# Chunked attention and a top-2 expert layer: two heads in one 128-row product, values loaded a batch ahead, routing work moved on VectorE

## The chip, the cores and the metric

One core of a Trainium2 chip runs the whole program. The metric is device time in microseconds (us) of one launch, from the program's start to its end; the median of several launches is given. A core has five engines that run side by side, each through its own stream of instructions in order: TensorE (PE in the profile; its weight loads are PEld), VectorE (DVE), ScalarE (ACT), GpSimd (POOL) and SyncE (SP). SP, ACT and POOL also issue DMA transfers. Waits between engines and transfers go through semaphores.

## What is computed

Attention in chunks (batch 4, 8 heads, 768 tokens, head width 64): each chunk of 32 queries sees 8 memory keys, 16 tokens to the left, its own 32 and 8 to the right, 64 keys in all. The result, seen as 3,072 rows of 512, goes through a layer of 8 experts of which each row takes the two best by noisy logits.

```python
for c in range(nc):                       # 24 chunks of 32
    k_full = np.concatenate([mem_k, k[:, :, l_start:r_end]], axis=2)
    v_full = np.concatenate([mem_v, v[:, :, l_start:r_end]], axis=2)
    scores = scale * np.matmul(q_c, k_full.transpose(0, 1, 3, 2))
    a = np.exp(scores - np.max(scores, axis=-1, keepdims=True))
    a = a / (np.sum(a, axis=-1, keepdims=True) + 1e-09)
    out[:, :, c_start:c_end] = np.matmul(a, v_full)
...
noisy_logits = x @ w_gate + np.log1p(np.exp(x @ w_noise)) * noise
top2 = np.argpartition(-noisy_logits, 2, axis=1)[:, :2]
...                                       # weights w of the two: softmax over them
    h = np.maximum(x[mask] @ w1[e], 0.0)
    out[mask] += top2_w[mask, k, None] * (h @ w2[e])
```

## The kernel before

**Two halves.** The attention half runs in 12 slots (`i` = 0 to 11): batch `b = i // 3`, and in it `tp = i % 3`, two tiles of 128 tokens. The expert half walks 20 visits of an expert to blocks of 128-row slots, with `mm1` (L637) and `mm2` (L652).

**One slot.** PE first makes the scores of the *next* slot (`scores`, L380): for each tile and each pair of heads a product against the memory keys and four against the windows, and all of these once for each head of the pair (`par`), with 64 rows of contraction. DVE takes the maximum and subtracts it (L406, L408), ACT takes the exponential (L413). Then PE turns this slot's probabilities (`turn_p`, L420), ACT copies them out (L423); PE turns the previous slot's rows (`turn_x`, L457); `values` (L426) makes the sums (L431) and the product with the values (L439), once for each head again; DVE takes the reciprocal (L444) and scales into `xrow` (L447). `gate` (L462) makes logits of the previous slot. `ps_s` and `ps_o` have one buffer each; the PSUM pool `psT`, for everything that is turned, has three.

**Keys, queries, values of the next batch.** In the slot with `tp == 1` PE turns the next batch's keys (four pairs, `turn`, L374, copies L546), in the one with `tp == 2` its queries (copies L528). Values take a longer way: they land in `vn`, POOL reorders them into `vp` (`spread_v`, L349), SP writes `vp` to DRAM (`vd`, L355), and POOL issues the loads of the windows back into `vb` (`window_v`: L359 for the memory values, L364 for the windows).

**POOL's queue.** All loads of v, k, q, windows and expert weights are issued by POOL, in the order of the program, on one DMA queue; a wait of one holds up those behind it. At `tp == 0` the order is `window_v(b+1)`, `load_batch(b+2)` (v, k, q), `spread_v(b+2)`. In the slots 6, 7 and 8 `load_expert(0)`, `(1)`, `(2)` follow, each two transfers (L74 for w1, L75 for w2).

**Memory.** The attention half borrows from `w_all`, which later holds the eight experts' weights, 8,192 elements of a partition each. `scratch` hands out pieces from the top down: `xrow`, `vb`, `vp`, `vn`, then `nat`, the raw k and q, [batch parity][k or q], of which `nat[1][1]` (q of batches 1 and 3) comes last and lowest. That is 36,864 of 65,536 elements, so the lowest piece starts at 28,672, in expert 3 (24,576 to 32,767).

**Order.** PE, ACT, DVE and SP follow the order of the program text as it is written in the main loop; POOL's are pinned. A read of `w_all` waits for the last write in program order that overlaps it.

**Routing.** `route(b)` (L326) is a generator of five steps: `choose` (18 small DVE operations, L224 to L258), `ranks` (PE) and `weights` (seven small DVE operations), `place` and `total`, `values` and `slots` (L311, L306), `lists`. The main loop takes a step at a time between the other stages. After slot 11 the last batch's routing follows in two parts, then rows are gathered by expert pair (L607) and the expert half starts.

Of the kernel before, what the change touches and what calls it, by code (L numbers as in the profile page):

```python
# [22 lines left out]
def kernel(  # L23
# [76 lines left out]
    vb = [scratch(NCH * HP * D).rearrange("p (c w) -> p c w", c=NCH) for _ in range(2)][::-1]  # L100
    vp = scratch(H * SO * D)
    vn = scratch(H * SO * D).rearrange("p (h c) -> p h c", h=H)
    nat = [[scratch(H * SO * D).rearrange("p (h c) -> p h c", h=H) for _ in range(2)] for _ in range(2)]
    first_late = scol[0] // WE

# [5 lines left out]
    def load_batch(b):  # L111
        load_nat(vn, v, b)
        load_nat(nat[b % 2][0], k, b)
        load_nat(nat[b % 2][1], q, b)

    load_batch(0)
# [13 lines left out]
    zeros = keep.tile([LC, Dm], BF16, name="zeros")  # L130
# [10 lines left out]
    mvs = keep.tile([B * NM, H, D], F32, name="mvs")  # L141
# [53 lines left out]
    kT = [keep.tile([128, HP, SP], BF16, name=f"kT{i}") for i in range(2)]  # L195
    qT = [keep.tile([128, HP, S], BF16, name=f"qT{i}") for i in range(2)]
    for i in range(2):
        nc.vector.memset(kT[i][:, :, 0:LC], 0.0)
        nc.vector.memset(kT[i][:, :, LC + S:SP], 0.0)

    mkT = keep.tile([128, HP, B * NM], BF16, name="mkT")
# [6 lines left out]
    nc.vector.tensor_copy(mkT, p_mk.rearrange("p c x b m -> p c (x b m)"))  # L208
# [117 lines left out]
    def route(b):  # L326
        r = Route(b * SO, SO, lgs[b])
        r.noise()
        yield
        advance(r.choose())  # L330
        yield
        r.ranks()
        r.weights(nc.vector)
        yield
        advance(r.place())
        advance(r.total())
        yield
        eng = nc.vector if b < B - 2 else nc.gpsimd
        r.values(eng, 0, NV)
        r.slots(nc.vector)  # L340
        yield
        r.lists(0, NV)
        yield


# [7 lines left out]
    def window_v(b):  # L353
        t, o = vb[b % 2], vd[b % 2]
        nc.sync.dma_start(out=o[LC:LC + S, :].rearrange("(p s) c -> p (s c)", s=SO), in_=vp)  # L355
        for par in range(2):
            p0 = par * 64
            cols = slice(par * 256, (par + 1) * 256)
            pin(nc.gpsimd.dma_start(out=t[p0:p0 + NM], in_=mvn[b * NM:(b + 1) * NM, cols].unsqueeze(1).to_broadcast([NM, NCH, 256])))  # L359
        for par in range(2):  # L360
            p0 = par * 64
            cols = slice(par * 256, (par + 1) * 256)
            for r0, n in ((0, CH), (CH, WIN - CH)):
                pin(nc.gpsimd.dma_start(out=t[p0 + NM + r0:p0 + NM + r0 + n],  # L364
                                        in_=o[r0:r0 + S, cols].rearrange("(c k) w -> k c w", k=CH)[0:n]))


    def turn(b, unit):
# [3 lines left out]
        for s in range(SO):  # L372
            for par in range(2):
                nc.tensor.transpose(out=p_t[par * 64:par * 64 + 64, s, :],  # L374
                                    in_=src[:, 2 * pair + par, s * D:(s + 1) * D],
                                    identity=identb, tile_position=(0, par * 64))
        dst = qT[b % 2][:, pair, :] if x else kT[b % 2][:, pair, LC:LC + S]
        return dst.rearrange("c (p s) -> c p s", s=SO), p_t.rearrange("c s p -> c p s")

    def scores(t):  # L380
        b, tp = divmod(t, TP)
        q_, k_ = qT[b % 2], kT[b % 2]
        ps_s = psS.tile([128, 2, 2, HP, KW], F32, name="ps_s")
        for j in range(2):
            for pair in range(HP):
                tk = (2 * tp + j) * 128
                for par in range(2):
                    rows = slice(par * 64, par * 64 + 64)
                    nc.tensor.matmul(out=ps_s[:, par, j, pair, 0:NM], lhsT=q_[rows, pair, tk:tk + 128],  # L389
                                     rhs=mkT[rows, pair, b * NM:(b + 1) * NM], start=True, stop=True,  # L390
                                     tile_position=(par * 64, 0))
                for r in range(4):
                    for par in range(2):
                        rows = slice(par * 64, par * 64 + 64)
                        tr = tk + r * CH
                        nc.tensor.matmul(out=ps_s[r * CH:(r + 1) * CH, par, j, pair, NM:KW],  # L396
                                         lhsT=q_[rows, pair, tr:tr + CH],
                                         rhs=k_[rows, pair, tr:tr + WIN], start=True, stop=True,
                                         tile_position=(par * 64, r * CH))
        if tp == 0:  # L400
            nc.vector.memset(ps_s[0:CH, :, 0, :, NM:NM + LC], NEG)
        if tp == TP - 1:
            nc.vector.memset(ps_s[128 - CH:128, :, 1, :, KW - RC:KW], NEG)
        s3 = ps_s.rearrange("p a j c w -> p (a j c) w")
# [6 lines left out]
    def exps(sc):  # L411
        pb = work.tile([128, 2 * HP, 2, KW], BF16, name="pb")
        nc.scalar.activation(out=pb.rearrange("p x a w -> p a x w"), in_=sc.rearrange("p (a x) w -> p a x w", a=2),  # L413
                             func=Act.Exp, scale=scale)
# [11 lines left out]
    def values(t, pT, between=None):  # L426
# [6 lines left out]
        ps_o = psO.tile([128, 2, 2, HP, D], F32, name="ps_o")  # L433
        for j in range(2):
            for pair in range(HP):
                for r in range(4):
                    for par in range(2):
                        rows = slice(par * 64, par * 64 + 64)
                        nc.tensor.matmul(out=ps_o[r * CH:(r + 1) * CH, par, j, pair, :],  # L439
                                         lhsT=pT[rows, j * HP + pair, r * CH:(r + 1) * CH],  # L440
# [457 lines left out]
```

## Time and profile before

| | |
|---|---|
| median of 3 runs | 391.89 us (388.24 to 396.87) |
| the profiled execution | 393.52 us, of which the profile's span is 391.8 us |
| busy in the span | PE 307.5, PEld 199.1, DVE 169.3, ACT 120.2, POOL 129.5 us |
| last rows of the attention half scaled (L447 of slot 11) | 151.9 us after the span's start |
| first gather of rows for the experts (L607) | 164.2 us |
| granted TensorE clock, mean | 0.85 |

Rows of the profile name line, engine, operation and "out<-in"; then how many, busy time and mean duration in ns, then the idle time before them and what ended it. In the timeline a row starts with its start and its duration in us, and [4.44 <-issue] means 4.44 us of idle time that ended with nothing that the profile shows. The slices cut the span into 40 parts of 9.8 us; a digit is a busy share in tenths. A row of the table of stretches gives each engine's busy time in that stretch, the clock, the DMA share and the GB/s moved. The trace also lists each DMA packet with queue, size, start and duration; v, k and q travel in packets of 768 bytes, windows in 4,096, w1 in 2,048 and w2 in 1,024, so each transfer can be followed by size.

### The profile page before, as it was taken

How to read it: one execution, taken by the hardware profiler on the slowest of the kernel's cores; microseconds unless marked ns; L12 is line 12 of the kernel's file. 1: busy time of each engine (PE TensorE's matmuls, PEld its weight loads, DVE VectorE, ACT ScalarE, POOL GpSimd, SP SyncE). 2: the span in 40 equal slices, each digit the busy share in tenths (PEclk: the TensorE clock that was granted, in tenths of full speed). 3: DMA queues.
4: the chain of work that ended last, by engine and by line, in shares of the span. 5: the costliest groups of instructions: out<-in, count | busy, mean ns of one | idle time of the engine just before them, and what ended most of it. 6: DMA issues, size and time to landing. Idle time of an engine off the chain costs nothing.

```text
span 391.8 us, 8846 instructions
## 1 busy us (share of the span) xinstructions
PE 307.5 (78%) x3868; PEld 199.1 (51%) x3868; DVE 169.3 (43%) x393; ACT 120.2 (31%) x182; POOL 129.5 (33%) x168
## 2 busy tenths in 40 slices
PE   0267765866758455379999999999988999999991
PEld 0256654755646343246555446666445666555540
DVE  2345444867657369734123411595321134313230
ACT  1122633540452323013432143312224411244310
POOL 6353234325520003476236522063272023201122
PEclk9999965565585555559999999999999999999997
DMA  9999999999999992039999970712039941100012
GB/s 125 238 141 189 213 157 222 219 150 217 204 182 218 217 205 66 12 98 190 240 209 247 228 153 14 122 44 95 24 114 173 210 97 73 68 5 2 21 43 74
DMA packets 42957, 54.07 MB, mean 138 GB/s; under 512 B 7607, under 2 KB 33271, under 8 KB 42912
## 3 DMA queue, kind: packets, MB, share of 16 engines
q0 software_dynamic: 34240, 46.82, 66.1%
q10 hardware_dynamic: 7136, 3.02, 3.6%
q1 hardware_dynamic: 1536, 3.61, 2.5%
q8 instruction: 32, 0.52, 0.5%
q14 instruction: 13, 0.11, 0.1%
HBM read 70.39 MB, written 13.96 MB: 215 GB/s over the span
## 4 chain that ended last, share of the span: by engine, by line
PE 30%; issue 17%; DMA 5%; POOL 4%; DVE 3%; POOLq 1%
PE p_h L646 16%; PE p_y L655 12%; DMA out_dram<-y,main_dst 5%; POOL out_dram L613 2%; PE p_xt L627 1%; POOL xt L607 1%; DMA xt<-xd,main_src 1%; POOL w_all L771 0%; POOL w_all L770 0%; DVE w_all L447 0%; POOLq L893 0%; DVE oh_l L306 0%; DVE c L227 0%; DVE mm L224 0%; DVE c L229 0%
## 5 line engine op out<-in xcount | busy, mean ns | idle before, releaser
L655 PE MATMUL p_y<-w_all,h 128*128 128x512 bf16 x464 | 103.9, 379 | 2.4 <-ACT y L659 2.4
L646 PE MATMUL p_h<-xTt,w_all 128*128 128x384 bf16 (+2 forms) x640 | 102.3, 319 | 0.0
L646 PEld LDWEIGHTS <-w_all 128*128 128x128 bf16 x704 | 66.8, 99 | 38.0 <-issue 2.1
L634 ACT ACTIVATE h<-p_h 128x512 bf16<-128x512 f32 (+1 forms) x82 | 44.7, 545 | 102.9 <-PE p_h L646 90.7
L655 PEld LDWEIGHTS <-h 128*128 128x128 bf16 x464 | 44.9, 98 | 53.5 <-issue 2.7
L632 DVE TENSOR_SCALAR h<-p_h 128x512 bf16<-128x512 f32 (+1 forms) x50 | 31.3, 626 | 89.4 <-PE p_h L646 86.4
L613 POOL DMA_INDIRECT out_dram<-y,main_dst x28 | 31.1, 1110 | 104.1 <-DVE y L661 84.0
L661 DVE SCALAR_TENSOR_TENSOR y<-p_y,main_w,y 128x512 f32<-128x512 f32 x28 | 21.0, 750 | 37.4 <-PE p_y L655 32.3
L607 POOL DMA_INDIRECT xt<-xd,main_src x28 | 27.3, 975 | 25.4 <-PE p_xt L627 16.1
L396 PE MATMUL ps_s<-kT,qT 64*32 64x56 bf16 x768 | 24.3, 220 | 13.3 <-issue 13.3
L374 PE MATMUL p_t<-identb,w_all 128*64 128x128 bf16 x384 | 20.8, 295 | 15.4 <-DMA w_all<-in_k_dram 8.2
L659 ACT ACTIVATE y<-p_y,main_w 128x512 f32<-128x512 f32 x28 | 19.1, 687 | 41.0 <-PE p_y L655 35.1
L423 ACT COPY pT<-p_p 128x1024 bf16<-128x1024 bf16 x12 | 12.1, 1012 | 58.2 <-PE p_p L420 58.2
L374 PEld LDWEIGHTS <-w_all 128*64 128x64 bf16 x384 | 18.7, 160 | 16.5 <-DMA w_all<-in_k_dram 8.3
L349 POOL COPY w_all<-w_all 128x1536 bf16<-128x1536 bf16 x8 | 13.0, 1658 | 35.0 <-DMA w_all<-in_v_dram 35.0
L389 PE MATMUL ps_s<-mkT,qT 64*128 64x8 bf16 x192 | 17.9, 184 | 4.4 <-DVE sc L408 2.9
L364 POOL DMA_DIRECT2D w_all<-vd x16 | 11.9, 748 | 25.0 <-DMA vd<-w_all 25.0
L406 DVE TENSOR_REDUCE mx<-ps_s 128x16 f32<-128x1024 f32 x12 | 14.7, 1223 | 8.9 <-PE ps_s L396 8.6
L447 DVE TENSOR_TENSOR w_all<-ps_o,rs 128x512 bf16<-128x512 f32 x24 | 15.6, 686 | 6.6 <-PE ps_o L439 6.0
L439 PE MATMUL ps_o<-w_all,pT 64*32 64x64 bf16 x768 | 10.0, 233 | 9.8 <-issue 9.8
L396 PEld LDWEIGHTS <-qT 64*32 64x32 bf16 x768 | 11.8, 96 | 11.2 <-issue 9.6
L389 PEld LDWEIGHTS <-qT 64*128 64x128 bf16 x192 | 10.0, 100 | 14.2 <-issue 5.8
(163 smaller groups left out, 300.3 us busy)
## 6 DMA issues: line engine op xcount, KB each, us to landing
w_all<-in_moe_w_dram POOLq DMA_DIRECT2D x16, 1024.0 KB
w_all<-in_moe_w_dram POOLq DMA_DIRECT2D x8, 512.0 KB
w_all<-in_v_dram POOLq DMA_DIRECT2D x4, 768.0 KB
w_all<-in_k_dram POOLq DMA_DIRECT2D x4, 768.0 KB
w_all<-in_q_dram POOLq DMA_DIRECT2D x4, 768.0 KB
vd<-w_all SPq DMA_DIRECT2D x4, 768.0 KB, 7.4
w_all<-vd POOLq DMA_DIRECT2D x8, 384.0 KB
xd<-w_all ACTq DMA_DIRECT2D x11, 256.0 KB, 7.6
```

The costliest lines, as they stand in the source:

```text
L374: nc.tensor.transpose(out=p_t[par * 64:par * 64 + 64, s, :], in_=src[:, 2 * pair + par, s * D:(s + 1) * D], identity=identb, tile_position ...
L389: nc.tensor.matmul(out=ps_s[:, par, j, pair, 0:NM], lhsT=q_[rows, pair, tk:tk + 128], rhs=mkT[rows, pair, b * NM:(b + 1) * NM], start=True ...
L396: nc.tensor.matmul(out=ps_s[r * CH:(r + 1) * CH, par, j, pair, NM:KW], lhsT=q_[rows, pair, tr:tr + CH], rhs=k_[rows, pair, tr:tr + WIN], s ...
L447: nc.vector.tensor_tensor(out=xr[:, j, 0:Dm].rearrange("p (c a d) -> p a c d", c=HP, a=2), in0=ps_o[:, :, j], in1=bc(rs[:, j].rearrange("p ...
L607: i = nc.gpsimd.indirect_dma_start(out=xts[key].bitcast(I32), out_offset=None, in_=xd, in_offset=bass.IndirectOffsetOnAxis(ap=ix, axis=0))
L613: i = nc.gpsimd.indirect_dma_start(out=out, out_offset=bass.IndirectOffsetOnAxis(ap=ix, axis=0), in_=y, in_offset=None, bounds_check=N - 1 ...
L632: nc.vector.tensor_scalar(out=out_, in0=in_, scalar1=0.0, scalar2=None, op0=Alu.max)
L634: nc.scalar.activation(out=out_, in_=in_, func=Act.Relu)
L646: nc.tensor.matmul(out=o, lhsT=w(kp * F + f * 128, 128), rhs=x[:, kp], start=(kp == 0), stop=(kp == KP - 1))
L655: nc.tensor.matmul(out=p, lhsT=h[:, (f * n + j) * 128:(f * n + j + 1) * 128], rhs=w(KP * F + f * Dm, Dm), start=(f == 0), stop=(f == FB - 1))
L659: nc.scalar.activation(out=y, in_=p, func=Act.Copy, scale=weight)
L661: nc.vector.scalar_tensor_tensor(out=y, in0=p, scalar=weight, in1=y, op0=Alu.mult, op1=Alu.add)
```

## The change

**Products.** Keys are kept block-diagonal: `kT` gets a column block for each head of a pair, with zeros in the other head's 64 rows; so do `mkT` and `vb`, whose size doubles. One product with 128 rows of contraction then serves both heads: per slot 40 instead of 80 in `scores`, with 112 instead of 56 columns (16 instead of 8 for the memory keys), and 32 instead of 64 in `values`, with 128 instead of 64 columns. A turned key tile is copied in two halves of 64 partitions. `kT` and `qT` have one buffer each instead of two. The zeros are written once at the start by DVE and ACT.

**Loads.** `load_batch` is split. `load_v(2)` is issued after `spread_v(1)`, before the loop, and `load_v(b + 3)` at `tp == 0` behind `spread_v(b + 2)`. `vp` leaves `w_all` for a tile of its own, `mvs` moves into expert 0's place.

**Memory.** The borrowed pieces now take 46,080 elements, and the lowest, `nat[1][1]`, lies at 19,456 to 22,527: inside expert 2 (16,384 to 24,575), the first 1,024 elements in w1's part, the rest in w2's. The calls of `load_expert` stay as they were, `load_expert(2)` in slot 8 ahead of the turn of batch 3's queries in the same slot. So in program order that turn reads what `load_expert(2)` has written there instead of batch 3's queries, and as built its first group of transposes waits for w1 of expert 2 and the second for w2.

**Routing.** `route` goes; its steps stand in the loop behind each slot's scaled rows and logits. `choose` is cut in two (8 and 10 operations, slots `tp == 0` and `tp == 1`), `weights` and `values` come ahead of the scores of the slot `tp == 2`, `settle` behind its logits, `lists` one slot later. In slot 11 `weights` and `values` are POOL's.

```diff
-    vb = [scratch(NCH * HP * D).rearrange("p (c w) -> p c w", c=NCH) for _ in range(2)][::-1]
-    vp = scratch(H * SO * D)
     vn = scratch(H * SO * D).rearrange("p (h c) -> p h c", h=H)
+    vb = [scratch(2 * NCH * HP * D).rearrange("p (a c w) -> p a c w", a=2, c=NCH) for _ in range(2)][::-1]
     nat = [[scratch(H * SO * D).rearrange("p (h c) -> p h c", h=H) for _ in range(2)] for _ in range(2)]
     first_late = scol[0] // WE
+    mvs = w_all[0:B * NM, 0, 0:2 * H * D].bitcast(F32).rearrange("p (h d) -> p h d", h=H)
...
-    def load_batch(b):
+    def load_v(b):
         load_nat(vn, v, b)
+
+    def load_kq(b):
         load_nat(nat[b % 2][0], k, b)
         load_nat(nat[b % 2][1], q, b)
...
+    vp = keep.tile([128, H * SO * D], BF16, name="vp")
+    zeros = keep.tile([128, Dm], BF16, name="zeros")
...
+    kT = keep.tile([128, HP, 2, SP], BF16, name="kT")
+    qT = keep.tile([128, HP, S], BF16, name="qT")
+    for par in range(2):
+        nc.vector.memset(kT[own(par), :, 1 - par, :], 0.0)
+        nc.vector.memset(kT[own(par), :, par, 0:LC], 0.0)
+        nc.vector.memset(kT[own(par), :, par, LC + S:SP], 0.0)
+        nc.vector.memset(vb[0][own(par), 1 - par], 0.0)
+        nc.scalar.copy(vb[1][own(par), 1 - par].rearrange("p (x c) w -> p x (c w)", x=NCH // 2),
+                       zeros[own(par), :].unsqueeze(1).to_broadcast([64, NCH // 2, Dm]))
+    mkT = keep.tile([128, HP, 2, B * NM], BF16, name="mkT")
...
     def turn(b, unit):
...
+        i = p_t.rearrange("c s p -> c p s")
+        if x:
+            return [(qT[:, pair, :].rearrange("c (p s) -> c p s", s=SO), i)]
+        return [(kT[own(par), pair, par, LC:LC + S].rearrange("c (p s) -> c p s", s=SO), i[own(par)]) for par in range(2)]
...
     def scores(t):
...
-                for par in range(2):
-                    rows = slice(par * 64, par * 64 + 64)
-                    nc.tensor.matmul(out=ps_s[:, par, j, pair, 0:NM], lhsT=q_[rows, pair, tk:tk + 128],
-                                     rhs=mkT[rows, pair, b * NM:(b + 1) * NM], start=True, stop=True,
-                                     tile_position=(par * 64, 0))
+                nc.tensor.matmul(out=ps_s[:, j, pair, :, 0:NM], lhsT=qT[:, pair, tk:tk + 128],
+                                 rhs=mkT[:, pair, :, b * NM:(b + 1) * NM], start=True, stop=True)
                 for r in range(4):
...
+                    tr = tk + r * CH
+                    nc.tensor.matmul(out=ps_s[r * CH:(r + 1) * CH, j, pair, :, NM:KW], lhsT=qT[:, pair, tr:tr + CH],
+                                     rhs=kT[:, pair, :, tr:tr + WIN], start=True, stop=True, tile_position=(0, r * CH))
...
     def values(t, pT, between=None):
...
                 for r in range(4):
-                    for par in range(2):
-                        rows = slice(par * 64, par * 64 + 64)
...
+                    nc.tensor.matmul(out=ps_o[r * CH:(r + 1) * CH, j, pair], lhsT=pT[:, j * HP + pair, r * CH:(r + 1) * CH],
+                                     rhs=vb[b % 2][:, :, (tp * 2 + j) * 4 + r, pair * D:(pair + 1) * D],
+                                     start=True, stop=True, tile_position=(0, r * CH))
...
         for u in range(2 * HP):
-            o_, i_ = turn(0, u)
-            (nc.scalar.copy if u % 2 else nc.vector.tensor_copy)(o_, i_)
-        load_batch(1)
+            for n, (o_, i_) in enumerate(turn(0, u)):
+                (nc.scalar.copy if (u + n) % 2 else nc.vector.tensor_copy)(o_, i_)
+        load_v(1)
+        load_kq(1)
         spread_v(1)
+        load_v(2)
...
             if tp == 0 and b + 1 < B:
                 window_v(b + 1)
                 if b + 2 < B:
-                    load_batch(b + 2)
+                    load_kq(b + 2)
                     spread_v(b + 2)
+                if b + 3 < B:
+                    load_v(b + 3)
             if i in range(2 * TP, 2 * TP + 3):
                 load_expert(i - 2 * TP)
-            if tp == TP - 1 and b + 1 < B:
-                for u in range(HP, 2 * HP):
-                    o_, i_ = turn(b + 1, u)
-                    (nc.scalar.copy if u % 2 else nc.vector.tensor_copy)(o_, i_)
-            if i + 1 < NT:
+            if tp == TP - 1:
+                if b + 1 < B:
+                    for u in range(HP, 2 * HP):
+                        o_, i_ = turn(b + 1, u)[0]
+                        (nc.scalar.copy if u % 2 else nc.vector.tensor_copy)(o_, i_)
+                if b:
+                    if last:
+                        r.ranks()
+                    r.weights(nc.gpsimd if last else nc.vector)
+                    r.values(nc.gpsimd if last else nc.vector, 0, NV)
+            if not last:
                 sc = scores(i + 1)
...
             pTs[i] = turn_p(pbs.pop(i))
             if i:
                 keep_x(i - 1, nc.scalar)
                 xTs_[i - 1] = turn_x(xrs.pop(i - 1))
+            if last:
+                advance(r.settle())
+            xrs[i] = values(i, pTs.pop(i), (lambda: gate(i - 1, xTs_.pop(i - 1))) if last else None)
+            if last:
+                break
+            pbs[i + 1] = exps(sc)
+            if tp == TP - 1 and b:
+                r.ranks()
+            if i:
+                gate(i - 1, xTs_.pop(i - 1))
+            if tp == TP - 1 and b:
+                advance(r.settle())
+            if tp == 0 and b > 1:
+                r.lists(0, NV)
+            if tp == 0 and b:
+                r = Route((b - 1) * SO, SO, lgs[b - 1])
+                r.noise()
+                chosen = r.choose()
+                advance(chosen, 8)
+            if tp == 1 and b:
+                advance(chosen)
             if tp == 1 and b + 1 < B:
                 for u in range(HP):
-                    o_, i_ = turn(b + 1, u)
-                    nc.scalar.copy(o_, i_)
+                    for o_, i_ in turn(b + 1, u):
+                        nc.scalar.copy(o_, i_)
```

## The prediction

> **What bounds the kernel now.** I read the slices first, for the stages:
>
> ```profile
> PE   0267765866758455379999999999988999999991
> PEclk9999965565585555559999999999999999999997
> DMA  9999999999999992039999970712039941100012
> ```
>
> Attention is slices 0 to 15 (to 152 us), routing 15 to 16, experts from 17 on, where PE is at 9. In attention PE is at 4 to 8 at half clock, while the DMA engines are full. The table of stretches says how full:
>
> ```profile
> 46.00:50.00 4.00, 3.89 (x90) 3.44 (x90) 1.92 (x2) 1.77 (x3) 3.18 (x5) 1.00 0.61 152
> 50.00:74.00 24.00, 14.89 (x482) 12.14 (x484) 12.38 (x25) 8.28 (x10) 6.64 (x7) 0.54 1.19 205
> 74.00:77.00 3.00, 3.00 (x64) 2.83 (x59) 2.69 (x11) 2.16 (x4) 1.82 (x3) 0.50 0.45 109
> 77.00:100.00 23.00, 15.30 (x425) 12.72 (x421) 15.06 (x29) 8.77 (x11) 9.52 (x9) 0.57 1.23 199
> 100.00:106.00 6.00, 5.01 (x153) 4.03 (x153) 4.32 (x11) 2.72 (x5) 3.41 (x5) 0.50 0.85 143
> 106.00:150.00 44.00, 27.32 (x753) 22.85 (x752) 27.84 (x79) 16.46 (x20) 5.65 (x7) 0.58 1.09 202
> 150.00:165.00 15.00, 4.90 (x66) 3.24 (x49) 12.70 (x59) 1.90 (x5) 4.92 (x16) 0.50 0.06 19
> ```
>
> The last figure is GB/s: about 200 wherever the queue is fed, less in three short gaps. The waits name the gaps, windows that wait for `vd`, and the timeline shows POOL issuing expert 2 last:
>
> ```profile
> POOL w_all L364 <- DMA vd<-w_all: 25.0, 4, 7.2
> ...
> 109.51 0.76 POOL L74 DMA_DIRECT2D w_all<-in_moe_w_dram  x1 [0.62 <-DMA w_all<-vd]
> 112.12 0.90 POOL L75 DMA_DIRECT2D w_all<-in_moe_w_dram  x1 [1.85 <-DMA w_all<-vd]
> ```
>
> By the DMA packets, taken apart by size, windows of batch 3 end at 115.97 us and expert 2's w2 at 149.90: 33.9 us for three experts. Nothing waits for that now; the experts start after 164. PE, meanwhile, stops with nothing to wait for:
>
> ```profile
> 61.32 0.24 PE L396 MATMUL ps_s<-kT,qT 64*32 64x56 bf16 x6 [4.44 <-issue]
> ...
> 89.84 0.52 PE L439 MATMUL ps_o<-w_all,pT 64*32 64x64 bf16 x38 [3.83 <-issue]
> ```
>
> There are 13 such stops between 22 and 150 us, 25.9 us in all, and each lies a multiple of 256 PE rows from the last, about 2 us behind a 16 KB packet of the instruction queue: PE runs out of code. The end of attention is DVE's, in the chain of waits:
>
> ```profile
> 151.69 0.17 DVE rs L444
> 151.85 0.09 issue
> 151.94 0.69 DVE w_all L447
> ```
>
> From there to the first gather (164.2) and through the experts I take everything as rigid: same code, same order.
>
> **Part 1, the overlap with expert 2, sets the end.** In slot 8 PE's turn of batch 3's queries now waits for w1 and w2 of expert 2, and reads their bytes. Queued behind it on PE: scores(9), then turn_p(8), values(8) and all that follows. Before, the same turn ran at 110.5 to 113.5. So the question is when w2 lands, and what follows it.
>
> *Landing.* The bytes ahead of it on the queue are those of before, so I start from 149.9. The values a batch ahead fill the gaps: at 205 GB/s the stretches 46 to 50, 74 to 77 and 100 to 106 lose 4 x (1 - 152/205) + 3 x (1 - 109/205) + 6 x (1 - 143/205) = 4.2 us. The `xd` writes of slots 9 to 11, 3 x 0.26 MB = 0.79 MB or 3.8 us at 205, come after the wait instead of before. 149.9 - 4.2 - 3.8 = 141.9; as a little of 100 to 106 was a queue refilling, I take 141. Bounds: 146 if no gap closes; 135 if all 27.6 MB up to there (9.4 of v, k, q, 3.1 of `vd`, 6.3 of windows, 2.1 of `xd`, 6.3 of experts, 0.4 of the rest) move at 205 from 0 us on.
>
> POOL does not hold the load back: batch 3's windows need values(5), behind batch 2's queries, which land about 74 us as now; expert 2's w2 also needs the key turn of slot 7, about 97.
>
> *After it.* Three groups of transposes (12 in 0.69 us each) and the last DVE copy, 2.5 us; then on DVE `weights` and `values`, now ahead of the scores' maximum, 1.4 (147.47 to 148.7 in the timeline) + 1.2, and the memset: the maximum of slot 9's scores starts 5.5 us after the landing. PE's scores(9), 2.4 us (eight blocks of 0.30, as from 54.43 to 54.73 in the timeline), lie beside this. Then DVE sets the pace, with 4.2 us a slot from these rows (1.2 + 1.2 + 0.25 + 2 x 0.69 + 0.18 for L471, less overlap):
>
> ```profile
> L447 DVE TENSOR_TENSOR w_all<-ps_o,rs 128x512 bf16<-128x512 f32 x24 | 15.6, 686 | 6.6 <-PE ps_o L439 6.0
> L408 DVE TENSOR_TENSOR sc<-ps_s,mx 128x1024 f32<-128x1024 f32 x12 | 14.7, 1225 | 1.0
> L406 DVE TENSOR_REDUCE mx<-ps_s 128x16 f32<-128x1024 f32 x12 | 14.7, 1223 | 8.9 <-PE ps_s L396 8.6
> ```
>
> Slot 8 adds settle (0.32 + 0.33 + 0.43 + 0.19 + 0.95 = 2.2), slot 9 `lists` and eight operations of `choose` (0.33 + 8 x 0.24 = 2.2), slot 10 ten (1.9), slot 11 ranks on PE (0.6) and settle (2.2): 5.5 + 6.4 + 6.4 + 6.1 + 2.8 = 27.2 us to slot 11's reciprocal, at 141 + 27.2 = 168.2 instead of 151.69. That is +16.5. Bounds of this stretch: 25, if half of the small operations fit into DVE's waits; 33, with code stops: some 900 PE rows remain, 3.5 blocks of 256 at 25.9/18 = 1.4 us each, 18 being the blocks that PE began between 22 and 150. I take none of these, as DVE has the pace and the queues are empty.
>
> The Trainium skill (Runtime: NRT & Kernel Launch, Instruction fetch mechanics) has such a block's crossing "mostly hidden". By it the stops cost nothing here either, the sum stays at +16.5 and the end at 33 would fall; the trace, with 13 stops in 18 blocks, disagrees.
>
> **Part 2, all that comes before slot 8, is worth nothing, because part 1's wait covers it.** Products: 72 fewer a slot, with their weight loads 1,728 PE rows, or 6.75 blocks; at 1.4 us about 9.7 us if PE set the pace. Values a batch ahead take away POOL's 35.0 us at L349, which were idle time of POOL; v of batch 2 now goes ahead of batch 1's windows, 4.1 us of packets, and these are needed only in slot 3 (64 us). Key copies in two halves: 12 more of 812 ns on ACT in the loop, 9.7 us, 3.2 a batch. Zeros at the start: 9,312 words a partition on DVE (two of 3,072, two of 1,584), 11 us by the 168-word memset of 0.20 us; 2 x 6,144 elements on ACT, 12.8 us by 0.80 for 768. DVE is idle there for 6.1 and ACT for 12.8 us; the first key copies move from 14.4 to about 18 us. Without cover this would cost 3 us once and 3.2 a batch, some 13 in all; but PE waited 1.49 us at 46.0 for batch 1's queries, and would reach slot 8 at about 97, 38 us ahead of w1. One buffer of `kT` and `qT`: the copies follow the scores that read the old ones, in order, at no cost. PE is idle before the landing, so the clock of what follows stays at the 0.50 that slots 9 to 11 had anyway.
>
> **The sum.** 393.52 + 16.5 = 410.0 for an execution like the profiled one, which stands 0.4% above the median of 391.89; 408.4 by the median. I predict 410.
>
> **The rivals.**
>
> *Packing lost, slower still.* Two 64-row products side by side become one of 128 rows that streams twice the columns, half of them against zeros. Now 64 products of 64 columns take 0.74 us at half clock (L439), 11.6 ns each, less than one alone could: the strips overlap. With 128 rows they may overlap less. Eight score products of 56 columns now start within 0.18 us (54.55 to 54.73 in the timeline), 22 ns each; four of 112 columns then take from 0.09 us, at 22 ns each, to 0.36, at twice the columns and with no second row half beside them, so a slot's scores 1.7 to 3.9 us and its values 0.37 to 3. Four slots at up to 3.8 more make 15, of which DVE's pace hides some 5: ten over the forecast, 420. For it: nothing in the trace has four strips with 128 rows. Against: 11.6 ns. TensorEngine Tiling (Array Packing), When to Use Tiling, of the Trainium skill would keep two row tiles for contractions up to 64, so it speaks against this part. Chance 0.10.
>
> *The queue runs faster, no change.* With w2 at 124.5 the end is where it was: 27.6 MB by then is 222 GB/s. For it: up to 240 where `vd` writes lie beside loads. Against: 202 over 44 us of expert loads. 392, chance 0.08.
>
> *The words of the change, faster.* If the slot-8 turn found its data in time, PE would set the pace: -9.7 for blocks, -4.2 for the queue's gaps, +5 of the 13 for copies and zeros that L423's waits on PE leave uncovered: 393.5 - 9 = 384. Point of decision: w2 down by 116 us. Against it: the three experts alone take 33.9 us and are issued behind batch 3's windows. Also possible if the wait does not bite at all. Chance 0.06.
>
> **How the numbers follow.** Forecast 0.76, the rivals 0.10, 0.08, 0.06. Range: 135 + 25 = 160 gives +8.5, or 402 (400 by the median); 146 + 33 = 179 gives +27, or 420. So 400 to 420, which leaves out the two lower rivals and part of the upper one, under 2 in 10. Two per cent is 7.8 us, so up to 399.7 it is "within": faster 0.06, within 0.09, slower 0.85.
>
> **What would show it.** In the changed profile: PE idle some 35 to 40 us before the query turn of slot 8, released by the expert weights; w2's last packet at about 141; no stop of PE for code of over 2 us behind it; DVE's L406 to L408 of slots 9 to 11 about 6.3 us apart; slot 11's reciprocal near 168 and 12.5 us from there to the first gather; 864 matmuls and 864 weight loads fewer; L349 without a wait after batch 1. Wrong I would be if PE's long wait is not there or ends on something else, if w2 lands before 130, or if the expert half, which I take as rigid, changes its length.

## The result, and the profile after

The changed kernel takes 413.63 us (410.51 to 416.84, four runs) beside 392.79 us for the kernel before on the same chip (four runs): a ratio of 1.0545, interval 1.0403 to 1.0686. Its profiled execution took 410.51 us, of which the span is 408.9. The slices first:

```profile
PE   0267799799300298536999999999999999999990
PEclk9999999999855566555999999999999999999997
DMA  9999999999999701103999996262125991100011
```

A slice is now 10.2 us. In slices 10 to 13, counted from 0 (102 to 143 us), PE is at 3, 0, 0 and 2 while the DMA engines are at 9, 9, 9 and 7; in the next two PE is at 9 and 8 and the DMA engines at 0 and 1. The timeline of PE names what it waited for (start, duration, row, idle time before it and what ended that):

```profile
136.81 0.96 PE L367 MATMUL p_t<-identb,w_all 128*64 128x128 bf16 x13 [30.41 <-DMA w_all<-in_moe_w_dram]
141.88 2.13 PE L367 MATMUL p_t<-identb,w_all 128*64 128x128 bf16 x35 [4.11 <-DMA w_all<-in_moe_w_dram]
```

These are the turns of batch 3's queries in slot 8: 30.4 us for w1 of expert 2, whose last packet ends at 136.50, and 4.1 more for w2, at 141.56. What follows is DVE's (timeline of DVE; maximum of the scores of slots 9, 10 and 11, then slot 11's reciprocal):

```profile
147.08 1.23 DVE L392 TENSOR_REDUCE mx<-ps_s 128x16 f32<-128x1024 f32 x1
...
153.54 1.22 DVE L392 TENSOR_REDUCE mx<-ps_s 128x16 f32<-128x1024 f32 x1
...
160.43 1.23 DVE L392 TENSOR_REDUCE mx<-ps_s 128x16 f32<-128x1024 f32 x1
...
169.47 0.26 DVE L426 RECIPROCAL rs<-ps_g 128x16 f32<-128x16 f32 x1 [0.18 <-PE ps_g L416]
```

The reciprocal was at 151.69, so the attention half is 17.8 us longer; the first gather is at 182.75 instead of 164.23, and from there to the end it is 226.1 us, 227.6 before. The table of stretches shows the queue's gaps (last column GB/s; it was 152, 109 and 143 in the first three) and DVE at 32 of 38 us after the wait:

```profile
46.00:50.00 4.00, 2.82 (x50) 2.49 (x48) 0.32 (x2) 3.62 (x6) 3.02 (x5) 1.00 1.46 231
74.00:77.00 3.00, 2.54 (x44) 2.21 (x41) 2.17 (x11) 2.64 (x5) 0.92 (x1) 1.00 1.26 239
100.00:106.00 6.00, 5.33 (x103) 4.70 (x103) 5.28 (x15) 4.69 (x6) 2.55 (x3) 1.00 1.04 165
145.00:183.00 38.00, 25.11 (x425) 19.37 (x421) 32.12 (x109) 13.21 (x18) 6.72 (x22) 0.59 0.10 36
```

Busy time alone would not have told: PE's rose by 7.8 us, with 864 matmuls and as many weight loads fewer (3,868 before):

```profile
PE 315.3 (77%) x3004; PEld 200.1 (49%) x3004; DVE 178.2 (44%) x395; ACT 143.4 (35%) x198; POOL 129.0 (32%) x174
```
Stops of PE for code, 25.9 us before, are gone from the waits up to 150 us. POOL's copies L342, which was L349, wait twice, and no longer 35.0 us in four waits (waits: total, times, longest):

```profile
POOL vp L342 <- DMA w_all<-in_v_dram: 14.0, 2, 11.1
```

### The profile page after: what moved, and what is told of

Its sections match the earlier page's. It is cut to its first block, busy times and chain, and to the rows that moved or that the text cites. A ratio compares the mean times of both kernels' runs of the same rounds, so it can differ in the third digit from the quotient of the medians.

```text
span 408.9 us, 7142 instructions
## 1 busy us (share of the span) xinstructions
PE 315.3 (77%) x3004; PEld 200.1 (49%) x3004; DVE 178.2 (44%) x395; ACT 143.4 (35%) x198; POOL 129.0 (32%) x174
## 4 chain that ended last, share of the span: by engine, by line
PE 31%; issue 16%; DMA 5%; POOL 4%; DVE 3%; POOLq 1%; ACT 0%
PE p_h L643 16%; PE p_y L652 12%; DMA out_dram<-y,main_dst 5%; POOL out_dram L610 2%; PE p_xt L624 1%; POOL xt L604 1%; DMA xt<-xd,main_src 1%; DVE w_all L429 1%; ACT pT L408 0%; PE ps_o L422 0%; PE p_p L405 0%; POOL w_all L768 0%; PE ps_s L384 0%; POOL w_all L767 0%; POOLq L890 0%
## 5 line engine op out<-in xcount | busy, mean ns | idle before, releaser
L367 PE MATMUL p_t<-identb,w_all 128*64 128x128 bf16 x384 | 24.3, 309 | 54.6 <-DMA w_all<-in_moe_w_dram 34.5
L367 PEld LDWEIGHTS <-w_all 128*64 128x64 bf16 x384 | 20.6, 168 | 57.5 <-DMA w_all<-in_moe_w_dram 34.9
L604 POOL DMA_INDIRECT xt<-xd,main_src x28 | 27.2, 972 | 25.4 <-PE p_xt L624 16.2
L384 PE MATMUL ps_s<-kT,qT 128*32 128x112 bf16 x384 | 26.8, 270 | 0.0
L515 DVE COPY qT<-p_t 128x768 bf16<-128x768 bf16 x6 | 5.7, 958 | 45.4 <-PE p_t L367 45.4
L380 PE MATMUL ps_s<-mkT,qT 128*128 128x16 bf16 x96 | 18.5, 192 | 2.9 <-DVE sc L394 2.9
L552 ACT COPY kT<-p_t 64x768 bf16<-64x768 bf16 x24 | 19.0, 793 | 1.6 <-PE p_t L367 1.2
L515 ACT COPY qT<-p_t 128x768 bf16<-128x768 bf16 x6 | 4.8, 798 | 32.8 <-PE p_t L367 32.6
```

Of the source, the lines that this page charges most:

```text
L367: nc.tensor.transpose(out=p_t[own(par), s, :], in_=src[:, 2 * pair + par, s * D:(s + 1) * D], identity=identb, tile_position=(0, par * 64))
L384: nc.tensor.matmul(out=ps_s[r * CH:(r + 1) * CH, j, pair, :, NM:KW], lhsT=qT[:, pair, tr:tr + CH], rhs=kT[:, pair, :, tr:tr + WIN], start= ...
L552: nc.scalar.copy(o_, i_)
L604: i = nc.gpsimd.indirect_dma_start(out=xts[key].bitcast(I32), out_offset=None, in_=xd, in_offset=bass.IndirectOffsetOnAxis(ap=ix, axis=0))
```

## The experiments

My theory was the prediction's: the wait for expert 2 sets the end and covers everything ahead of slot 8. Its rival: the parts themselves are slower, or the wait only stands where another would. A ratio is to runs of the kernel before on the same chip; the three sets of four ran on three chips, on which that took 393.49, 396.32 and 398.83 us, so ratios are what can be compared.

| kernel | median us | ratio to before | interval |
|---|---|---|---|
| the change | 413.63 | 1.0545 | 1.0403 to 1.0686 |
| e2, overlap alone | 420.31 | 1.0721 | 1.0621 to 1.0821 |
| e1, change with expert 2 loaded behind the turn | 379.45 | 0.9664 | 0.957 to 0.9758 |
| e12, e1 again | 384.47 | 0.9687 | 0.9625 to 0.9749 |
| e6, products alone | 381.57 | 0.9727 | 0.9642 to 0.9813 |
| e5, loads and routing with the old products | 399.28 | 1.0194 | 1.0096 to 1.0292 |
| e7, values ahead alone | 400.72 | 1.0103 | 1.006 to 1.0146 |
| e8, routing alone | 395.36 | (see below) | |
| e3, e1 without values ahead | 381.9 | 0.9616 | 0.9553 to 0.9679 |
| e4, e1 with the old routing | 385.87 | 0.9722 | 0.967 to 0.9773 |
| e10, e1, one reordering on ACT | 385.07 | 0.9691 | 0.9629 to 0.9752 |
| e9, e1, copies shared, zeros later | 385.69 | 0.9662 | 0.9592 to 0.9733 |
| e11, e9 without values ahead | 383.47 | 0.9624 | 0.9554 to 0.9693 |

### The overlap, taken away and put in alone (e1, e2)

e1 is the change with one call moved behind the turn that reads what lies there:

```diff
-            if i in range(2 * TP, 2 * TP + 3):
+            if i in range(2 * TP, 2 * TP + 2):
                 load_expert(i - 2 * TP)
             if tp == TP - 1:
                 if b + 1 < B:
...
+                if i == 2 * TP + 2:
+                    load_expert(2)
```

> The changed kernel with one call moved: load_expert(2) stands behind the turn of batch 3's queries in slot 8, so the turn reads the queries and the load waits for the turn. Theory (the wait for expert 2's weights is the whole loss): PE no longer idles before that turn; it came there at 106.4 us in the changed kernel, and 28 us later follows slot 11's reciprocal, at about 135 to 140 instead of 169.5; the first gather at 148 to 153, but its rows queue behind w2 of expert 2, which lands at about 145; with the 226 us from the first gather to the end, 375 to 382 us. Rival (the 128-row products are slower themselves, eight score blocks now 0.34 us each against 0.30): 392 us or more.

e2 is the kernel before with one line, which puts `nat` where the change puts it; as in the change, batch 3's queries are then read from expert 2's bytes:

```diff
     xrow = [scratch(SO * Dm).rearrange("p (s r) -> p s r", s=SO) for _ in range(2)]
     vb = [scratch(NCH * HP * D).rearrange("p (c w) -> p c w", c=NCH) for _ in range(2)][::-1]
     vp = scratch(H * SO * D)
     vn = scratch(H * SO * D).rearrange("p (h c) -> p h c", h=H)
+    scratch(9216)
```

> The kernel before with nothing changed but 9,216 elements of w_all left out ahead of nat, so that nat[1][1] comes to lie at 19,456, inside expert 2, as in the changed kernel; batch 3's queries are then read from expert 2's bytes. Theory: the loss is the overlap's alone, PE idles in slot 8 until w2 of expert 2 has landed, at about 146 (149.9 less the three xd writes that now come later), and some 30 us follow to slot 11's reciprocal: 176 instead of 151.7, so 412 to 420 us, as slow as the changed kernel or slower. Rival (the loss needs the products or the new order): within 1% of the kernel before.

e1 took 379.45 us and e2 420.31: both as the theory has it. The timeline of PE of e2:

```profile
140.52 0.95 PE L375 MATMUL p_t<-identb,w_all 128*64 128x128 bf16 x13 [29.73 <-DMA w_all<-in_moe_w_dram]
145.59 1.49 PE L375 MATMUL p_t<-identb,w_all 128*64 128x128 bf16 x23 [4.11 <-DMA w_all<-in_moe_w_dram]
```

The same wait, in a kernel that has nothing else of the change, makes it slower by as much or more. And without the wait the change is faster than before by 3.4%. So the overlap alone turns the sign: 1.0545 / 0.9664 = 1.09, about the 34.5 us that PE stands still. e2 also takes the landing apart: its w2 ends at 145.25, 4.7 us earlier than before with no value loaded ahead (the `xd` writes come after the wait); the change's ends 3.7 us earlier still. From the wait's end to slot 11's reciprocal e2 needs 31.6 us (145.59 to 177.16), the change 27.6.

### The products alone, and the rest alone (e6, e5)

e6 is the kernel before with the products, their zeros and copies, the change's place of its pieces in memory, and expert 2 loaded behind the turn as in e1; loads of values and routing are as before. e5 is the other way round: the new loads and routing with the old 64-row products, and memory as before, so without overlap. The heart of e6:

```diff
-                for r in range(4):
-                    for par in range(2):
-                        rows = slice(par * 64, par * 64 + 64)
...
-                                         rhs=k_[rows, pair, tr:tr + WIN], start=True, stop=True,
-                                         tile_position=(par * 64, r * CH))
+                for r in range(4):
+                    tr = tk + r * CH
+                    nc.tensor.matmul(out=ps_s[r * CH:(r + 1) * CH, j, pair, :, NM:KW], lhsT=qT[:, pair, tr:tr + CH],
+                                     rhs=kT[:, pair, :, tr:tr + WIN], start=True, stop=True, tile_position=(0, r * CH))
```

> Only the 128-row products of the change (block-diagonal keys and values, key copies in halves, zeros at the start), with loads and routing as before and load_expert(2) behind the turn of batch 3's queries. Theory (PE stops for code are what the products take away): the 13 stops of 25.9 us mostly go, each slot pays 0.3 us more for scores and 0.3 for values, so 8 us given back, and key copies some 5: 10 to 15 us faster than before, 377 to 384 us. Rival (packing lost, no stop saved that was on the path): 392 us or more.

> The kernel before with the two other parts of the change, values a batch ahead and the new place of the routing, but its own 64-row products (nothing overlaps expert 2 then). Theory: PE's code stops stay and keep the pace; the queue's gaps of 4 us and some DVE waits go: 384 to 391 us. Rival (the queue or DVE had the pace, not PE's code): under 382 us, as fast as the whole change without its wait.

e6 took 381.57 us, in the theory's range: nearly all of e1's gain is the products'. e5 took 399.28, outside of both ranges and slower than before: the new loads and routing are no gain of their own. What differs most between the two traces are the stops of PE for code. All that is left of them in e6's attention half, from its waits between 20 and 150 us (total, times, longest), and the longest in e5, from its timeline:

```profile
PE p_t L388 <- issue: 0.2, 1, 0.2
```

```profile
114.55 0.23 PE L379 MATMUL ps_s<-kT,qT 64*32 64x56 bf16 x3 [8.97 <-issue]
```

In e5 there are 14 stops with 32.9 us in all (13 with 25.9 before). The one of 8.97 us began at 105.6, and its 16 KB packet of the instruction queue ran only at 111.99, behind 4,096-byte packets of batch 3's windows. That the windows hold the code up is read from this order and not shown by a run.

### Which of the two costs (e7, e8, e3, e4)

e7 is the kernel before with only the loads changed, e8 with only the routing moved. The edit of e7; undone in e1, it makes e3:

```diff
-        load_batch(1)
+        load_v(1)
+        load_kq(1)
         spread_v(1)
+        load_v(2)
...
-                    load_batch(b + 2)
+                    load_kq(b + 2)
                     spread_v(b + 2)
+                if b + 3 < B:
+                    load_v(b + 3)
```

> The kernel before with nothing changed but the values of a batch loaded a batch ahead. Old products with new loads and routing took 399.28 us, 6 more than before, with 14 stops of PE for code of 32.9 us instead of 13 of 25.9, one of 8.97 us that began at 105.6 us while the code packet came only at 111.99, behind windows of batch 3. Theory: more loads stand in the queue beside the windows, the code comes later, and this alone costs: 395 to 403 us, stops of 29 us or more, one of them over 6 us. Rival A (gaps of the queue closed, as the prediction's lower rival has it): 385 to 391, stops as before. Rival B (the routing costs it): 390 to 395, stops of 23 to 28 us.

> The kernel before with nothing changed but the place of the routing's steps. Theory (the loads cost it, by code that comes late): 390 to 395 us, stops of PE for code of 23 to 28 us in all. Rival (the routing costs it, as DVE's small operations now stand ahead of the maximum of the next slot's scores in slots 5, 8 and 11): 396 to 402, with stops as before and DVE as the releaser of PE's waits there.

> The products and the new place of the routing, expert 2 loaded behind the turn, values loaded as before (v with k and q of its batch). It stands between the kernel with all three (379.45 us) and the one with the products alone (381.57), which differ by 2.1 us. Theory: without code stops the values a batch ahead still close the queue's gaps, and slot 8's queries land some 2 us earlier for it, so without them 380 to 384. Rival: the gain over the products alone is the routing's, then 377 to 380. Neither expects the stops of PE for code to come back: at most 2, under 3 us in all.

> The products and the values a batch ahead, expert 2 loaded behind the turn, routing at its old place. Theory (the values ahead are what gains with the new products): 377 to 381. Rival (the routing is): 381 to 385. If the 399.28 us of old products with new loads and routing came from the routing's new place by itself, whatever the products are, this one must be about 10 us faster than 379.45; neither theory has that.

e7 took 400.72 us beside 396.32, so the loads alone cost 1.0% (0.6 to 1.5). The theory's reason failed, though: its stops are 11 with 23.1 us in all, none over 5.94. e8 took 395.36 us beside 396.32; its runs spread from 388.29 to 398.87, and its stops, 28.9 us, are about as before: no cost that can be told, and neither expectation was met (395.36 lies between the two ranges). e3 and e4 took 381.9 and 385.87 us, ratios of 0.9616 and 0.9722: of what e1 has over the products alone, the routing is the larger part (0.9722 to e1's 0.9664 and 0.9687; 0.9727 to 0.9616 without values ahead; the intervals overlap), and the values ahead gain nothing. Their expected ranges were in us of the first chip, where before took 393.49; these ratios make 378.4 and 382.5 us of it, in both cases the rival's range, the routing's. In e4 PE waits 4.06 and 1.40 us for DVE's reciprocal in slots 10 and 11; e1 waits 2.81 us for DVE's `ohp` in slot 11 instead.

e7's timelines show where part of its cost is, first DVE's, then POOL's:

```profile
79.74 3.46 DVE L277 TENSOR_TENSOR d<-mm 128x6 f32<-128x6 f32 x1
```

```profile
79.40 0.90 POOL L109 DMA_DIRECT2D w_all<-in_q_dram  x1 [4.31 <-DMA w_all<-in_v_dram]
80.29 2.88 POOL L352 COPY w_all<-w_all 128x1536 bf16<-128x1536 bf16 x2
```

A DVE operation whose median is 0.16 us ends at 83.20, and POOL's two copies of batch 3's values end at 83.17. Behind it DVE's query copy is late, and PE waits 2.79 us for that at 85.2. Values ahead have moved POOL's copies into this place.

### The lock and the uncovered costs (e12, e10, e9, e11)

e12 is e1 once more, as a companion on the same chip. e10 gives the reordering of batch 3's values to ACT, in slot 5 behind the query copies:

```diff
+            if b == B - 1:
+                nc.scalar.copy(o_, i_)
+            else:
+                pin(nc.gpsimd.tensor_copy(out=o_, in_=i_))
```

> The whole change with expert 2 loaded behind the turn, once more, on the same chip as the next three so that they can be set against it: a ratio to before of 0.957 to 0.976, as in its first run, is expected by every theory.

> As the companion, but batch 3's values are reordered by ACT, behind the query copies of slot 5, instead of by POOL. In the kernels with values ahead POOL's two copies (2.88 us together) run at about 81 us and a DVE operation of 0.16 us with two inputs from SBUF takes until POOL is done (81.18 to 83.98 in the first run of the companion, 79.74 to 83.20 with the values ahead alone); with values loaded as before POOL does them elsewhere. Theory: POOL's copies shut DVE out, and that is what the values ahead cost: the operation takes under 0.4 us and the time falls by 1 to 2.6 us against the companion. Rival 1: the operation waits for something else and stays over 2 us. Rival 2: it is gone, but ACT's two copies or the rest of the slot take its place: within 1 us of the companion.

The companion repeats e1. In e10 the operation is short again; timelines of DVE of e12 and e10, then of ACT of e10:

```profile
81.86 3.54 DVE L287 TENSOR_TENSOR d<-mm 128x6 f32<-128x6 f32 x1
```

```profile
83.66 0.16 DVE L287 TENSOR_TENSOR d<-mm 128x6 f32<-128x6 f32 x1
```

```profile
84.46 2.85 ACT L345 COPY vp<-w_all 128x1536 bf16<-128x1536 bf16 x2
87.46 1.01 ACT L411 COPY pT<-p_p 128x1024 bf16<-128x1024 bf16 x1
```

So POOL's copies did shut DVE out. But the time is 385.07 us beside the companion's 384.47: ACT's copies of 2.85 us now stand ahead of its copy of slot 5's probabilities. Rival 2 holds: the wait moved.

e9 makes the start and the key copies cheaper, and e11 is e9 with e7's edit undone:

```diff
-        nc.vector.memset(vb[0][own(par), 1 - par], 0.0)
-        nc.scalar.copy(vb[1][own(par), 1 - par].rearrange("p (x c) w -> p x (c w)", x=NCH // 2),
+        nc.scalar.copy(vb[0][own(par), 1 - par].rearrange("p (x c) w -> p x (c w)", x=NCH // 2),
...
+        nc.vector.memset(vb[1][own(0), 1], 0.0)
...
+        nc.vector.memset(vb[1][own(1), 0], 0.0)
...
-                    for o_, i_ in turn(b + 1, u):
-                        nc.scalar.copy(o_, i_)
+                    for n, (o_, i_) in enumerate(turn(b + 1, u)):
+                        (nc.vector.tensor_copy if n else nc.scalar.copy)(o_, i_)
```

> As the companion, with the two costs that the prediction put under the wait made smaller: of each turned key tile ACT copies one half and DVE the other, and the zeros of the first value buffer are ACT's, those of the second are written by DVE behind batch 0's queries and scores. Theory (in the version without the wait these costs are not covered: the first turn of probabilities at 35 instead of 30.5 us, PE waits of 1.1 us for ACT's key copies): the first turn at 30 to 32 us, the waits at L554 gone, 4 to 8 us faster than the companion. Rival: later work sets the end (loads of keys and queries, DVE's pace), the head start is lost by slot 3, within 1.5 us of the companion.

> As the kernel with shared copies, but with values loaded as before. If the values ahead cost something with the new products too (0.9664 with them against 0.9616 without, on different chips), it is 1 to 3 us faster than the kernel with shared copies; if they gain (gaps of the queue closed), 1 to 3 us slower; within 1 us, they do nothing.

e9 took 385.69 us: no gain, as its rival has it. Its first turn of probabilities came at 32.7 us instead of 35.0, and the head start grew to 3.7 us by slot 3 (58.5 beside 62.2), where it was lost. PE's waits for ACT's key copies are gone, but 4.1 us for DVE's halves stand in their place. PE's timeline of e9 and of e11 at slot 3's values:

```profile
65.91 1.14 PE L421 MATMUL ps_o<-w_all,pT 128*32 128x128 bf16 x32 [4.81 <-DMA w_all<-vd]
```

```profile
61.01 1.05 PE L421 MATMUL ps_o<-w_all,pT 128*32 128x128 bf16 x32
```

In e9 the windows of batch 1 end at 64.67, behind 7 us of batch 2's values; in e11 these come later and the windows end at 59.14. e11 took 383.47 us, 2.2 less than e9, as a cost of the values ahead would have it, though these two intervals overlap. The sign was the same with the old products (e7), with the new ones (e3 beside e1) and here; only e7's interval leaves out no effect. e11 and e3 have the lowest ratios, near 0.962, 9% below the change; their intervals overlap those of e1, e12 and e9.

## Why the prediction held, step by step

**The result and the rivals.** 410.0 was said for an execution like the profiled one, which took 410.51. That the two lie so close is in part luck: it is the fastest of four, whose median of 413.63 is 20.8 us above the kernel before, where 16.5 were said; the two profiled spans differ by 17.1. (The range's lower end, 160 less 151.69, is +8.3 and not +8.5, which changes nothing.) The first rival, packing lost (420), is refuted by e6; the queue faster (392) by w2 at 141.56; the words of the change (384) came near as soon as the load stood behind the turn (e1: 0.9664 of 393.52 is 380), though not by that rival's terms, as is said below.

**Landing.** Said 141, measured 141.56. Its terms: 3.8 us for the `xd` writes, measured 4.7 in e2; 4.2 for the gaps of the queue, and the change's w2 is 3.7 ahead of e2's.

**After it.** Said 27.2 us to slot 11's reciprocal, measured 27.6; maxima said 6.3 us apart, measured 6.5 and 6.9; reciprocal said near 168, measured 169.47. From there to the gather 13.3 instead of 12.5. That DVE alone has the pace there is not shown. From the first maximum (147.1 us) to slot 10's scaling (163.2) DVE is idle for 1.6 us, but PE for only 1.9; between the first two maxima, 6.5 us apart, DVE is busy for 5.9 us and PE for 6.2; and from 156.30 to 163.17 the chain that ended last runs through PE and ACT. A sum of PE's work would have come out about the same, so the 6.3 that fits does not prove the step. The granted clock was 1.00 instead of 0.50 from 150 to 157 us, which the sum did not have. No stop of PE for code came behind the wait; of the two reasons that the forecast gave, the empty queues are borne out by e2, see below.

**Where PE was when the wait began.** Said about 97 us, measured 106.4. The start cost 4.8 us instead of the 3 that I gave it: the first turn of probabilities moved from 30.5 to 35.3 us, and in e9, with the zeros spread, 2.3 us of this are gone. PE waited for ACT's key copies, 4.3 us in seven waits in the change and 7.2 in nine in e1. What the rest of the 9.4 us is made of, no run takes apart. It made the wait 34.5 instead of 35 to 40 us and changed nothing in the sum, which is what "covered" means.

**Part 2 worth nothing.** Right in the change: PE came to the turn at 106.4 us in it and at 110.8 in e2, and in both it then stood until w1 had landed. (The 7.7 us by which the change's reciprocal of slot 11 comes ahead of e2's lie in the landing, 3.7, and behind the wait, 4.0.) Without the wait, what comes before slot 8 is worth little too: that query turn ends at 112.35 us in e1 and at 113.46 in the kernel before. Nearly all of e1's 13.8 us to slot 11's reciprocal (137.8 for 151.6) is gained behind it.

As prices without the cover, two terms of the third rival were wrong. *Blocks, -9.7 us*: mis-sized. I took the stops off in proportion to the instructions (6.75 blocks at 1.4 us); but in e6 all but 0.2 of 25.9 us went, and the kernel gained 2.7% (1.9 to 3.6) with the zeros and copies paid. One reason is the rate: a score block issued 20 PE rows in 0.30 us before and 10 in 0.34 us now, so a block of 256 rows lasts twice as long, and the next one arrives within it. That it is the rate is argued from the rows, not tried. The other reason is the queues, and e2 shows it: with the old products at the old rate it has no stop behind its wait, where the DMA engines carry little. This is the stretch from the end of slot 8's query turn to slot 11's reciprocal, in one profiled execution each:

| kernel | products | us | GB/s moved | stops of PE for code |
|---|---|---|---|---|
| before | old | 38.2 | 195 | 5, 10.7 us |
| e2 | old | 29.0 | 39 | none |
| e6 | new | 29.7 | 206 | none |
| e1, routing moved too | new | 25.5 | 220 | none |
| the change, routing moved too | new | 25.5 | 39 | none |

Of the first two, the rows in the table of stretches, the kernel before and then e2:

```profile
113.46:151.61 38.15, 22.00 (x629) 18.03 (x630) 23.30 (x57) 11.91 (x14) 1.88 (x1) 0.55 1.05 195
148.18:177.16 28.98, 21.19 (x629) 17.97 (x630) 22.49 (x56) 11.90 (x14) 1.88 (x1) 0.50 0.11 39
```

So in these runs the stops need the old products and full queues together. In the times of the packets, the next 16 KB of code started 3.6 to 7.1 us after PE had begun a block in that stretch of the kernel before, and at most 1.1 us after it in e2; that the loads in the queues delay it is read from this and was not tried by itself. The Trainium skill's "mostly hidden" (Runtime: NRT & Kernel Launch, Instruction fetch mechanics) fits the new rate, where e1 has one stop of 1.18 us, and the old rate over nearly idle queues, but not the old rate over full ones.

*Gaps, -4.2 us*: wrong sign. The queue's gaps did close, but the transfer that filled them stood ahead of windows that PE needed next (e9, 4.81 us), and its reordering on POOL shut DVE out. "Needed only in slot 3 (64 us)" had no slack as soon as PE came earlier.

**Packing.** At half speed a block of scores costs 0.34 instead of 0.30 us, the values of a slot 1.05 instead of 0.74 us: 0.6 us more a slot, where up to 3.8 was feared. The slot's scores then take 2.7 us, in the middle of their bounds (1.7 to 3.9), and the values lie near their lower end (0.37 to 3). The preference of the Trainium skill for two row tiles up to 64 rows (TensorEngine Tiling (Array Packing), When to Use Tiling) agrees with these rows alone; what it leaves out here is that half the instructions end the stops over full queues.

What stays open: how e5's 1.9% divides, since e7 and e8 give 1.0% and nothing that can be told; whether the windows cause the longest stops (e2 shows only that a nearly idle queue has none); and the size of the cost of values ahead with the new products.

## What to carry to other kernels

When pieces of memory are borrowed from a buffer that is loaded later, a bigger piece elsewhere can push one of them under an earlier load: read the new addresses against the load order before pricing anything else, because one such wait hides most of what the other edits do. A gain that is off the path in one version may be the whole gain in the next, so measure parts with the wait taken out. A load moved ahead fills idle time of its queue, but look at what it now stands in front of and at what else it triggers, on other engines too. Where an engine stops for code, look at how fast its instructions go by and at the queues together: here fewer instructions ended the stops, and so did idle queues.

## What the runs showed of the hardware

**DVE waits for POOL's copies.** In the change and in e1, e5, e7, e9 and e12, one DVE operation with two inputs in SBUF that began between 79.7 and 82.5 us took 2.3 to 3.5 us and ended 0.02 to 0.03 us behind POOL's second copy; query copies of 0.96 us, which read PSUM, ran unhindered beside POOL's copies in e4 (81.72 us). The Trainium skill has this lock (SBUF — State Buffer, SBUF: two separate sides): a DVE operation with two SBUF inputs and a POOL operation that reads SBUF exclude each other. The trace agrees, and adds that DVE did not get in between POOL's two copies. In four of the six the operation began some 0.6 us ahead of the copy's row, while POOL issued a transfer (L109); why it did not end there is open.

**PE runs at half speed nearly all through attention, and a mean granted clock hides this where the clock was not recorded.** In the change the trace's record of the granted clock begins at 105.8 us, and all before it counts as 1.00 in the slices and stretches. But a turn of probabilities (eight products) takes 1.03 us there, as it does at a recorded 0.50, and 0.62 only at 153, where 1.00 is recorded for 6.8 us. Timeline of PE of the change, slots 5 and 9:

```profile
84.47 1.03 PE L405 MATMUL p_p<-identb,pb 128*128 128x128 bf16 x8
...
152.90 0.62 PE L405 MATMUL p_p<-identb,pb 128*128 128x128 bf16 x8
```

e10's record begins only at 166.5 us, so its profiled run has 1.00 all the way from 50 to 150; its companion's begins at 73.4 and gives 0.70. The products of these turns are 107 ns apart nearly everywhere in both; the one slot of the companion with 56 ns, at 100 us, lies in a recorded stretch of 1.00. So the record, where there is one, agrees with the spacing, and such a mean over a stretch without a record is no measure of PE's speed; the spacing of like products is.
